# Row sums of the attention weights: one matmul group per head, or one per four heads after a fold by DMA

## The chip, the cores and the metric

The kernel runs on one core of a Trainium2 chip. The metric is the device time of one launch in microseconds (us). The core has five engines that run their own instruction streams and wait for each other by semaphores: PE (TensorE, matmuls), ACT (ScalarE), DVE (VectorE), POOL (GpSimd) and SP (SyncE, here only a queue that issues DMAs). Sixteen DMA engines move data for all queues.

## The reference

Two blocks work on the same x (2048 tokens, 1024 features) and a gate mixes them. Block A is attention with 32 heads of 32 features. Block B is a product-key expert layer. The change touches block A, and there the softmax alone.

```
g = sigmoid((x * gate_w).sum(-1, keepdims=True))
qkv = (x @ wqkv) in 3 parts, 32 heads, 32 features
scores = einsum("bhqd,bhkd->bhqk", q, k) * 32 ** -0.5
p = softmax(scores)          # exp, then divided by its sum over k
a = einsum("bhqk,bhkd->bhqd", p, v) reshaped @ wo
b = block B (keys, 8 x 8 experts, top 1)
out = g * a + (1 - g) * b
```

## The kernel before

Everything is in fp32, and where a matmul is made of two or three parts in a rounded fp32 format, in those. The first 640 us or so make q, k, v and block B's inner values and store them in HBM. The last 180 us or so multiply by wo. Between them lies the attention stage, which the change is about.

**Heads, tiles, steps.** The stage goes through 32 heads. A head's keys are cut into 16 tiles of 128 (`NT = 16`); the program calls tile `kt` of head `h` step `h * NT + kt`, and takes two steps at a time (`BT = 2`). For one step, `scores` (L968) makes four matmuls of 128 keys by 512 queries into banks of a ring of 7 PSUM banks (`ring`), and ACT takes the exponential of one to three banks at a time (L978) into an SBUF tile `P` of 128 keys by 2048 queries. Two steps later `pv` (L989) multiplies the tile by the head's values V into the PSUM bank `o`. The weight of these matmuls is 32 columns wide, so the four blocks of 512 queries go side by side, to partitions 0, 32, 64 and 96.

**Places of the tiles.** A `P` tile lives in one of eight places, `P0` to `P7`, in turn (`p_tile`). The exponential for a place waits until the tile that was there eight tiles earlier has been read by everybody.

**Row sums.** The division needs the sum of each P over all 2048 keys. Per head, `presum` adds the tiles up elementwise: tile 1 is written to `accd` directly, tiles 3, 8 and 12 are added to `accd` by accumulating DMAs that POOL issues (L1011), and DVE adds the eleven others to `acc` (L1016 and L1018). In the next head, at its step 5, `merge` adds `accd` to `acc` (L1021). At its step 8 `head_sums` sums over the 128 partitions: four matmuls with a 128 x 32 tile of ones into one bank of the ring (`rowsum`, L1002). ACT copies the bank to `ssb` (L1039), and SP stores one row of each 32 in HBM (`smd`). Once in four heads `load_r` and `norm_r` read the sums of the group back, take reciprocals times the gate (L1050, L1051) and store them (`rd`).

**The order.** It is written out by hand: the dictionary `todo` holds, for each step, the functions that run besides scores and pv. They are called after the two steps' scores and the earlier steps' pv, and before `presum` of their own step. Every engine, and every queue that issues DMAs, works in the order of the calls. SP's queue has in each head the store of the head before (`finish`, at step 0, out of `osb`), seven loads of the next head's K and Q (`load_head`, step 2), a piece of the next group's V (`load_v`, step 7) and, in heads 8 to 23, half of a row block of wo (step 11), which is needed only at the end of the kernel. POOL's queue has the three accumulating DMAs and nothing else.

**The pool `keep`.** It holds four tiles `wo_raw0` to `wo_raw3` for wo, `vhl` for block B's values and `rb0`, from before the first head on, each as large as a P tile: 8 KB in each of 128 partitions. In the heads before their loads they lie empty.

Of the kernel before, what the change touches and what calls it, by code (L numbers as in the profile page):

```python
# [9 lines left out]
F32 = mybir.dt.float32  # L10
F32R = mybir.dt.float32r
I32 = mybir.dt.int32
AF = mybir.ActivationFunctionType
OP = mybir.AluOpType
AX = mybir.AxisListType

S = 2048
D = 1024
H = 32
KC = D // 128  # L20
HC = KC // 2
NT = S // 128
NQ = S // 512
G = H // 4
W = 256
# [6 lines left out]
def gated_mha_peer_kernel(ctx, tc, xT, wqkv, wv, wo, wq, k12, ug, v, out):  # L32
# [8 lines left out]
    nc = tc.nc  # L41
# [3 lines left out]
    const = ctx.enter_context(tc.tile_pool(name="const", bufs=1))  # L45
# [10 lines left out]
    SMD = [dram.tile([4, S], F32, name=f"smd{g}") for g in range(G)]  # L56
# [3 lines left out]
    VPD = [dram.tile([128, D], F32R, name=f"vp{part}") for part in "hl"]  # L60
# [3 lines left out]
    ones = const.tile([128, 32], F32, name="ones")  # L64
# [8 lines left out]
    def dma(dst, src, queue=nc.sync):  # L73
        a, b = (ap.bitcast(F32) if ap.dtype == F32R else ap for ap in (dst, src))
        return queue.dma_start(a, b)
# [27 lines left out]
    def bank():  # L103
        i = bank_no[0] % 8
        bank_no[0] += 1
        return ps1.tile([128, 512], F32, name=f"bk{i}")
# [215 lines left out]
    for k, (w, c) in enumerate(chunks):  # L322
        hi, lo = whl.pop((w, c))
        for n in range(NQ):
            ps = bank()
# [9 lines left out]
            blk = 4 * k + n  # L335
# [16 lines left out]
            if blk >= 42 and blk < 50:  # L352
                kc = blk - 42
# [8 lines left out]

    blk = const.tile([128, 4], F32, name="blk")
    nc.vector.tensor_reduce(blk, ident.rearrange("p (j r) -> p j r", j=4), axis=AX.X, op=OP.max)
    pr = const.tile([128, KC], F32, name="pr")
    nc.vector.tensor_mul(pr, amax[:, 0, :], amax[:, 1, :])
    prm = const.tile([128, KC, 4], F32, name="prm")
# [427 lines left out]
    def values_unit(u):  # L795
# [10 lines left out]
        for k, name in enumerate(order):  # L806
# [6 lines left out]
            if last and name == "P2":  # L813
                first_scores()
# [41 lines left out]

    P, pools = {}, {}

    def p_tile(h, kt):

        i = pools["next"] % 8
        pools["next"] += 1
        P[h, kt] = pools["left" if i >= 4 else "right"].tile([128, S], F32, name=f"P{i}")
        return P[h, kt]

    def first_scores():

        tp.close()
        pools.update(right=Pool("ppr", side="right"), next=0)
        K, Q = Z  # L870
        pt = p_tile(0, 0)
        for qc, i in enumerate((5, 6, 0, 1)):
            ps = ps1.tile([128, 512], F32, name=f"bk{i}")
            c = slice(qc * 512, (qc + 1) * 512)
            nc.tensor.matmul(ps, K[:98, :128], Q[:98, c], start=True, stop=True)
            nc.scalar.activation(pt[:, c], ps, AF.Exp, scale=SCALE)
# [20 lines left out]
    xp.close()  # L897


    keep = Pool("keep")  # L900

    wo_raw = [keep.tile([128, 2, D], F32, name=f"wo_raw{i}") for i in range(KC // 2)]
    vhl = keep.tile([128, 2, D], F32R, name="vhl")
    rb0 = keep.tile([128, KC, W], F32, name="rb0")

    def raw_wo(kc):
        i, j = divmod((kc - 1) % KC, 2)
        return wo_raw[i][:, j]

    wk = Pool("wk", bufs=2)  # L910

    ACC = {0: wk.tile([128, S], F32, name="acc")}
# [10 lines left out]
    ring = pss.tile([128, NB, 512], F32, name="ring")  # L923
# [3 lines left out]
    def ring_banks(n):  # L927
        i = [(ring_no[0] + k) % NB for k in range(n)]
        ring_no[0] += n
        return i  # L930

    def on_ring(ins, *banks):

        for other, theirs in users:
            if ins.ins.engine != other.ins.engine and not theirs & set(banks):
                tc.declare_no_dep(ins.ins, other.ins, reason="different banks of the ring")
        users.append((ins, set(banks)))
        del users[:-6 * NB]
# [57 lines left out]

    SUMS = (1, 3, 8, 12), (2, 4, 6)

    def rowsum(ps, *srcs):
        for src in srcs:  # L1000
            for qc in range(NQ):
                yield nc.tensor.matmul(ps[32 * qc:32 * qc + 32, :], ones,  # L1002
                                       src[:, qc * 512:(qc + 1) * 512],
                                       start=(src is srcs[0]), stop=(src is srcs[-1]))

    def presum(h, kt):
        sums = SUMS[h == H - 1]
        if kt == 0 or kt == sums[0] or (h == H - 1 and kt >= NT - 2):
            return
        if kt in sums:  # L1010
            nc.gpsimd.dma_start(ACCD[h], P[h, kt], accum_op=OP.add)  # L1011
            return
        if kt == 1 + (sums[0] == 1):
            if h > 0:
                ACC[h] = wk.tile([128, S], F32, name="acc")
            nc.vector.tensor_add(ACC[h], P[h, 0], P[h, kt])  # L1016
        else:
            nc.vector.tensor_add(ACC[h], ACC[h], P[h, kt])  # L1018
# [4 lines left out]
    def head_sums(h):  # L1023
        i, = ring_banks(1)
        for ins in rowsum(ring[:, i, :], ACC.pop(h)):
            on_ring(ins, i)
        on_ring(norm_sums(h, ring[:, i, :]), i)

    def finish(h):
        g, j = divmod(h, 4)  # L1030
        o = wk.tile([128, 512], F32, name="osb")
        nc.scalar.activation(o, O.pop(h), AF.Copy)
        dma(OD[g][32 * j:32 * j + 32, :].rearrange("d (q s) -> q d s", q=NQ), o)


    def norm_sums(h, ps):
        g, j = divmod(h, 4)
        o = wk.tile([128, 512], F32, name="ssb")
        ins = nc.scalar.activation(o, ps, AF.Copy)  # L1039
        dma(SMD[g][j:j + 1, :].rearrange("o (q s) -> (o q) s", q=NQ), o[::32, :])  # L1040
        return ins
# [13 lines left out]
    OC, RB = {}, {}  # L1055
# [6 lines left out]

    def load_rb(n, k0, k1, js=range(4), queue=nc.sync):
        if k0 == 0 and js[0] == 0:
            RB[n] = rb0 if n == 0 else wk.tile([128, KC, W], F32, name="accd")
        for j in js:
            src = RD[k0:k1, j:j + 1, n * W:(n + 1) * W].rearrange("g j s -> j g s")
            dma(RB[n][32 * j:32 * j + 32, k0:k1, :], src.to_broadcast([32, k1 - k0, W]), queue)

    def load_chunk(n, k0, k1, queue=nc.sync):  # L1070
        load_o(n, k0, k1, queue)
        load_rb(n, k0, k1, queue=queue)
# [5 lines left out]
    def split_first(step):  # L1078
        o = OC[0][:, 0, :]
        if step == 0:  # L1080
            W0.append(zp.tile([128, 2, D], F32R, name="z1"))
            OH[0] = zp.tile([128, KC, W], F32R, name="z0")
            OL[0] = wk.tile([128, KC, W], F32R, name="acc")
            nc.vector.tensor_mul(o, o, RB[0][:, 0, :])
        elif step == 1:
            nc.scalar.activation(W0[0][:, 0], raw_wo(0), AF.Copy)
        elif step == 2:
            nc.scalar.activation(OH[0][:, 0, :], o, AF.Copy)
        else:
            for lo, src, hi in ((W0[0][:, 1], raw_wo(0), W0[0][:, 0]),  # L1090
                                (OL[0][:, 0, :], o, OH[0][:, 0, :])):
                nc.vector.tensor_tensor(out=lo, in0=src, in1=hi.bitcast(F32), op=OP.subtract)

    todo = {}

    def at(step, f, *a):
        todo.setdefault(step, []).append((f, a))

    for h in range(H):
        base = h * NT  # L1100
        g, j = divmod(h, 4)
        if h < H - 1:
            at(base + NT, finish, h)
            at(base + NT + 5, merge, h)
            at(base + NT + 8, head_sums, h)
        if j == 3 and g + 1 < G:
            at(base + NT + 10, load_r, g)
            at(base + NT + 14, norm_r, g)
        if h >= 1 and h + 1 < H:
            at(base + 2, load_head, h + 1)  # L1110
        if g + 1 < G:
            at(base + 7, load_v, g + 1, j)
# [1 line left out]
        at((H - 1) * NT + step, split_first, i)  # L1114
    at((H - 1) * NT + 13, merge, H - 1)
    for k in range(2 * KC):
        c = slice(k % 2 * D // 2, (k % 2 + 1) * D // 2)
        at((8 + k) * NT + 11, dma, raw_wo(k // 2)[:, c], wo[:, k // 2 * D:(k // 2 + 1) * D][:, c])
    for i in range(2):
        at(28 * NT + 6 + i, dma, vhl[:, i], VPD[i])  # L1120
    at(29 * NT + 13, load_o, 0, 0, 4)
    at(30 * NT + 7, load_o, 0, 4, KC - 1)
    at(30 * NT + 13, load_rb, 0, 0, KC - 1, range(2))
# [6 lines left out]
    for b0 in range(0, (H + 1) * NT, BT):  # L1130
# [9 lines left out]
        for k in range(b0, b0 + BT):  # L1140
            for f, a in todo.pop(k, []):
                f(*a)
            if now:
                presum(*now[k - b0])
    assert not todo
    pss.close()
    pools["left"].close()
    pools["right"].close()
# [29 lines left out]
    def av_mm(n, tt, half, ps, first=False, last=False):  # L1178
        for i in range(2):
            nc.tensor.matmul(ps, AT[n][:, tt * 128:(tt + 1) * 128],  # L1180
                             vhl[:, i, half * 512:(half + 1) * 512],
                             start=(first and i == 0), stop=(last and i == 1))

    bank_no = [0]
# [40 lines left out]
            nc.vector.tensor_mul(o, o, RB[n][:, k * HC:(k + 1) * HC])  # L1225
        ht.rows(OC[n])

    post = rb0.rearrange("p k m -> p (k m)").rearrange("p (a m) -> p a m", m=512)

    def plain_out(n, pa):  # L1230
        for i, ((j, half), ps) in enumerate(pa.items()):
# [44 lines left out]
    for (i, half), ps in pa.items():  # L1276
        av_mm(0, i, half, ps)
# [11 lines left out]
    for (i, half), ps in pa1.items():  # L1289
        av_mm(1, i, half, ps)  # L1290
# [127 lines left out]
```

## Time and profile before

| What | Value |
|---|---|
| median of 3 runs | 1856.39 us (1855.58 to 1862.57) |
| the profiled execution, time | 1856.62 us |
| its span, first to last instruction | 1854.8 us |
| instructions | 26123 |
| mean granted TensorE clock | 0.999 |
| PE busy | 1843.4 us, 99% |
| DVE busy | 1365.7 us, 74% |
| ACT busy | 1198.9 us, 65% |
| POOL busy | 170.1 us, 9% |

The profile is that of one execution. A row of groups has line, engine, operation, output <- inputs, shapes and count, then busy time and the mean duration of one in ns, then the idle time of the engine before them and what ended it. A row of the timeline has the start in us, the length in us, engine, line, operation and count, and in brackets the idle time before it and who ended it. A row of windows has for each engine its busy time in the stretch and the number of instructions, then the granted clock, the share of the 16 DMA engines' time that was busy, and GB/s. A row of waits has the waiting engine and line, whom it waited for, the total in us, how often, and the longest. "PEld" is the loading of weights into PE, which runs beside matmuls.

### The profile page before, as it was taken

The page shows a single profiled execution, that of the slowest core. Times are in us where ns is not written, and L with a number is a line of the kernel's source. Part 1 is how long each engine was busy: PE and PEld are TensorE (multiplying, and loading weights), DVE is VectorE, ACT ScalarE, POOL GpSimd, SP SyncE. Part 2 cuts the span into 40 slices and gives each one's busy share as a digit, 9 for nine tenths or more (in the row PEclk, how much of TensorE's full clock was granted, in tenths as well). Part 3 has the DMA queues.
Part 4 walks back from the last instruction along what each step waited for, and adds up shares of the span by engine and source line. Part 5 has one row for each costly group of instructions (what it writes and reads, how often), then busy time and mean ns, then how long its engine had stood idle before and what let it go on. Part 6 is the DMA issues. An engine that isn't in the chain of part 4 may idle for free.

```text
span 1854.8 us, 26123 instructions
## 1 busy us (share of the span) xinstructions
PE 1843.4 (99%) x10127; PEld 1130.9 (61%) x10127; DVE 1365.7 (74%) x1219; ACT 1198.9 (65%) x1492; POOL 170.1 (9%) x214
## 2 busy tenths in 40 slices
PE   9999999999999999999999999999999999999999
PEld 7877777887888744444444444444444444447787
DVE  4522224978887788888888888888888888895674
ACT  4211111201233399999999999999999999993221
POOL 0000000025401100000000000000000000000000
PEclk9999999999999999999999999999999999999999
DMA  5777784423237687767777777777777777766861
GB/s 215 281 251 255 273 290 135 134 66 104 80 127 247 246 182 160 177 153 176 163 175 176 163 183 170 184 160 183 172 172 169 159 176 177 182 147 196 273 171 57
DMA packets 122853, 332.10 MB, mean 179 GB/s; under 512 B 15988, under 2 KB 57220, under 8 KB 98472
## 3 DMA queue, kind: packets, MB, share of 16 engines
q1 hardware_dynamic: 85048, 180.58, 32.2%
q0 software_dynamic: 17584, 112.08, 28.0%
q10 hardware_dynamic: 20096, 37.76, 6.6%
q8 instruction: 80, 1.31, 0.3%
q14 instruction: 45, 0.37, 0.1%
HBM read 158.65 MB, written 72.10 MB: 124 GB/s over the span
## 4 chain that ended last, share of the span: by engine, by line
PE 85%; issue 6%; DMA 4%; DVE 3%; POOL 1%; ACT 1%; SPq 0%; ACTq 0%; DVEq 0%; POOLq 0%
PE ring L968 28%; PE o L989 25%; PE bk L329 17%; PE pa L617 6%; PE bk L394 3%; PE bk L213 2%; PE bk L274 2%; PE ring L1002 1%; DMA accd<-rd 1%; POOL eq L408 1%; PE pa L1180 1%; DMA t3l<-t2l 1%; DMA rb<-rd 1%; DMA t1l<-xl 1%; DMA smd<-ssb 0%
## 5 line engine op out<-in xcount | busy, mean ns | idle before, releaser
L978 ACT ACTIVATE P<-ring 128x1024 f32<-128x1024 f32 (+2 forms) x1031 | 913.0, 982 | 13.5 <-DMA accd<-P 1.2
L1018 DVE TENSOR_TENSOR acc<-acc,P 128x2048 f32<-128x2048 f32 x319 | 731.0, 2292 | 74.6 <-ACT P L978 49.0
L989 PE MATMUL o<-P,V 128*32 128x512 f32 x3840 | 464.8, 599 | 0.0
L968 PE MATMUL ring<-Q,K 98*128 98x512 f32 x1024 | 272.0, 407 | 0.1
L968 PE MATMUL ring<-z,z 98*128 98x512 f32 x1020 | 270.5, 407 | 0.6 <-ACT accd L978 0.6
L968 PEld LDWEIGHTS ring<-Q,K 98*128 98x128 f32 x1024 | 182.0, 188 | 144.2 <-ACT P L978 72.4
L968 PEld LDWEIGHTS ring<-z,z 98*128 98x128 f32 x1020 | 181.4, 188 | 142.5 <-ACT P L978 72.5
L989 PEld LDWEIGHTS o<-P,V 128*32 128x32 f32 x3840 | 98.8, 109 | 223.3 <-issue 214.4
L93 ACT ACTIVATE hi<-bk 128x512 fp32r<-128x512 f32 x64 | 37.6, 598 | 243.2 <-PE bk L329 227.1
L94 DVE TENSOR_TENSOR lo<-bk,hi 128x512 fp32r<-128x512 f32 x64 | 44.1, 690 | 182.7 <-ACT hi L93 178.5
L329 PE MATMUL bk<-xh,whi 128*128 128x512 f32 x448 | 176.2, 393 | 0.1
L329 PE MATMUL bk<-xh,wlo 128*128 128x512 f32 x448 | 174.4, 389 | 0.0
L329 PE MATMUL bk<-xl,whi 128*128 128x512 f32 x448 | 174.4, 389 | 0.0
L1011 POOL DMA_DIRECT2D accd<-P x95 | 81.5, 858 | 929.4 <-ACT P L978 421.4
L1016 DVE TENSOR_TENSOR acc<-P,P 128x2048 f32<-128x2048 f32 x32 | 73.4, 2293 | 72.9 <-ACT P L978 72.9
L329 PEld LDWEIGHTS bk<-xh,whi 128*128 128x128 f32 x448 | 84.1, 188 | 24.2 <-issue 6.7
L329 PEld LDWEIGHTS bk<-xh,wlo 128*128 128x128 f32 x448 | 84.1, 188 | 17.7
L329 PEld LDWEIGHTS bk<-xl,whi 128*128 128x128 f32 x448 | 84.2, 188 | 16.9
L1021 DVE TENSOR_TENSOR acc<-acc,accd 128x2048 f32<-128x2048 f32 x32 | 73.1, 2285 | 0.0
L978 ACT ACTIVATE accd<-ring 128x1024 f32<-128x1024 f32 (+2 forms) x64 | 62.2, 1032 | 2.5 <-PE ring L968 2.4
L617 PE MATMUL pa<-woh,acc 128*128 128x512 f32 x192 | 62.2, 389 | 0.0
L398 ACT ACTIVATE xu<-bk 128x64 f32<-128x64 f32 x16 | 3.6, 224 | 76.5 <-PE bk L394 71.6
(246 smaller groups left out, 1868.0 us busy)
## 6 DMA issues: line engine op xcount, KB each, us to landing
accd<-P POOLq DMA_DIRECT2D x95, 1024.0 KB, 7.5
wqt<-in_wq SPq DMA_DIRECT2D x32, 1024.0 KB
z<-kdh SPq DMA_DIRECT2D x32, 256.0 KB
z<-qdh SPq DMA_DIRECT2D x32, 256.0 KB
V<-vd SPq DMA_DIRECT2D x32, 256.0 KB
K<-kdh SPq DMA_DIRECT2D x32, 256.0 KB
Q<-qdh SPq DMA_DIRECT2D x32, 256.0 KB
od<-osb SPq DMA_DIRECT2D x32, 256.0 KB
```

Source lines behind the costliest of these rows:

```text
L93: nc.scalar.activation(hi, src, AF.Copy)
L94: (on or nc.vector).tensor_tensor(out=lo, in0=src, in1=hi.bitcast(F32), op=OP.subtract)
L329: nc.tensor.matmul(ps, a[:, kc, :], b[n][:, kc, :], start=first, stop=last)
L394: nc.tensor.matmul(ps, a[t // 4][:, kc, tok], b, start=first, stop=last)
L617: nc.tensor.matmul(ps, self.a[a][i][:, k, :], self.b[b][j][k], start=(not first and k == 0 and i == j == 0), stop=(k == HC - 1 and i == 1))
L968: on_ring(nc.tensor.matmul(ring[:, i, :], K[:98, kt * 128:(kt + 1) * 128], Q[:98, qc * 512:(qc + 1) * 512], start=True, stop=True), i)
L978: on_ring(nc.scalar.activation(P[h, kt][:, q0 * 512:(q0 + m) * 512].rearrange("p (a m) -> p a m", a=m), ring[:, i:i + m, :], AF.Exp, scale ...
L989: nc.tensor.matmul(O[h][32 * qc:32 * qc + 32, :], Vt[g][:, kt, 32 * j:32 * j + 32], p[:, qc * 512:(qc + 1) * 512], start=(kt == 0), stop=( ...
L1011: nc.gpsimd.dma_start(ACCD[h], P[h, kt], accum_op=OP.add)
L1016: nc.vector.tensor_add(ACC[h], P[h, 0], P[h, kt])
L1018: nc.vector.tensor_add(ACC[h], ACC[h], P[h, kt])
L1021: nc.vector.tensor_add(ACC[h], ACC[h], ACCD[h])
```

## The change

**The fold.** For heads 0 to 27 `head_sums` is no longer called. `halve`, at step 5 of the next head, is an accumulating DMA from POOL's queue that adds partitions 64 to 127 of `acc` to partitions 0 to 63 (512 KB). `quarter`, at step 10, has DVE copy partitions 0 to 31 of `acc` into 32 partitions of a tile `FOLD`, the head's number in its group of four choosing which 32. `add_quarter`, at step 11, is a second accumulating DMA, which adds partitions 32 to 63 of `acc` to them (256 KB). After four heads `FOLD` holds 32 partial sums of each, and `group_sums`, at step 2 of the second head after the group, makes the four matmuls once, with a weight `fours` of 128 x 32 that has eight equal columns for each head, and one copy by ACT and one store by SP. `load_r` and `norm_r` follow at steps 5 and 9 there. `merge` is at step 4 instead of 5. Heads 28 to 31 have their sums as before.

**The places.** The list `places` names for each tile its place: thirteen rounds of thirteen places (P0 to P7, `rb0` and the four `wo_raw`), then five rounds of twelve, six of eleven, six of ten, five of nine and ten of eight. `vhl`'s place is that of the `FOLD` tiles.

**The loads.** wo is loaded in heads 12 to 27 instead of 8 to 23, beginning with row block 1 and ending with block 0, and block B's values at step 6 of head 29 instead of head 28.

```diff
     nc.vector.tensor_reduce(blk, ident.rearrange("p (j r) -> p j r", j=4), axis=AX.X, op=OP.max)
+    fours = const.tile([128, 4, 8], F32, name="fours")
+    nc.vector.tensor_copy(fours, blk[:, :, None].to_broadcast([128, 4, 8]))
     pr = const.tile([128, KC], F32, name="pr")
...
+    places = []
+    for rounds, spare in ((13, 5), (5, 4), (6, 3), (6, 2), (5, 1), (10, 0)):
+        places += rounds * ([f"P{i}" for i in range(8)] +
+                            ["rb0", "wo_raw3", "wo_raw2", "wo_raw1", "wo_raw0"][:spare])
     def p_tile(h, kt):
-        i = pools["next"] % 8
-        pools["next"] += 1
-        P[h, kt] = pools["left" if i >= 4 else "right"].tile([128, S], F32, name=f"P{i}")
+        place = places.pop(0)
+        pool = pools["keep" if place[0] != "P" else "left" if place >= "P4" else "right"]
+        P[h, kt] = pool.tile([128, S], F32, name=place)
         return P[h, kt]
...
         tp.close()
-        pools.update(right=Pool("ppr", side="right"), next=0)
+        pools["right"] = Pool("ppr", side="right")
         K, Q = Z
...
-    keep = Pool("keep")
-    wo_raw = [keep.tile([128, 2, D], F32, name=f"wo_raw{i}") for i in range(KC // 2)]
-    vhl = keep.tile([128, 2, D], F32R, name="vhl")
-    rb0 = keep.tile([128, KC, W], F32, name="rb0")
+    keep = pools["keep"] = Pool("keep")
+    wo_raw = {}
+    FOLD = [keep.tile([128, S], F32, name="vhl")]
...
         i, j = divmod((kc - 1) % KC, 2)
+        if i not in wo_raw:
+            wo_raw[i] = keep.tile([128, 2, D], F32, name=f"wo_raw{i}")
         return wo_raw[i][:, j]
+    def load_wo(k):
+        kc, c = (k // 2 + 1) % KC, slice(k % 2 * D // 2, (k % 2 + 1) * D // 2)
+        dma(raw_wo(kc)[:, c], wo[:, kc * D:(kc + 1) * D][:, c])
...
-    def rowsum(ps, *srcs):
+    def rowsum(ps, *srcs, weights=ones):
         for src in srcs:
             for qc in range(NQ):
-                yield nc.tensor.matmul(ps[32 * qc:32 * qc + 32, :], ones,
+                yield nc.tensor.matmul(ps[32 * qc:32 * qc + 32, :], weights,
                                        src[:, qc * 512:(qc + 1) * 512],
...
+    def halve(h):
+        nc.gpsimd.dma_start(ACC[h][:64, :], ACC[h][64:, :], accum_op=OP.add)
+    def quarter(h):
+        g, j = divmod(h, 4)
+        if j == 0 and g > 0:
+            FOLD.append(keep.tile([128, S], F32, name="vhl"))
+        nc.vector.tensor_copy(FOLD[g][32 * j:32 * j + 32, :], ACC[h][:32, :])
+    def add_quarter(h):
+        g, j = divmod(h, 4)
+        nc.gpsimd.dma_start(FOLD[g][32 * j:32 * j + 32, :], ACC.pop(h)[32:64, :], accum_op=OP.add)
+    def group_sums(g):
+        i, = ring_banks(1)
+        for ins in rowsum(ring[:, i, :], FOLD[g], weights=fours.rearrange("p j r -> p (j r)")):
+            on_ring(ins, i)
+        o = wk.tile([128, 512], F32, name="ssb")
+        on_ring(nc.scalar.activation(o, ring[:, i, :], AF.Copy), i)
+        dma(SMD[g].rearrange("j (q s) -> q j s", q=NQ), o[::8, :])
+    vhl = []
+    def load_v_parts(i):
+        if i == 0:
+            vhl.append(keep.tile([128, 2, D], F32R, name="vhl"))
+        dma(vhl[0][:, i], VPD[i])
     def finish(h):
...
         if k0 == 0 and js[0] == 0:
-            RB[n] = rb0 if n == 0 else wk.tile([128, KC, W], F32, name="accd")
+            RB[n] = wk.tile([128, KC, W], F32, name="accd") if n else \
+                keep.tile([128, KC, W], F32, name="rb0")
         for j in js:
...
             at(base + NT, finish, h)
-            at(base + NT + 5, merge, h)
-            at(base + NT + 8, head_sums, h)
+            at(base + NT + 4, merge, h)
+            if g < G - 1:
+                at(base + NT + 5, halve, h)
+                at(base + NT + 10, quarter, h)
+                at(base + NT + 11, add_quarter, h)
+            else:
+                at(base + NT + 8, head_sums, h)
         if j == 3 and g + 1 < G:
-            at(base + NT + 10, load_r, g)
-            at(base + NT + 14, norm_r, g)
+            at(base + 2 * NT + 2, group_sums, g)
+            at(base + 2 * NT + 5, load_r, g)
+            at(base + 2 * NT + 9, norm_r, g)
         if h >= 1 and h + 1 < H:
...
     for k in range(2 * KC):
-        c = slice(k % 2 * D // 2, (k % 2 + 1) * D // 2)
-        at((8 + k) * NT + 11, dma, raw_wo(k // 2)[:, c], wo[:, k // 2 * D:(k // 2 + 1) * D][:, c])
+        at((12 + k) * NT + 11, load_wo, k)
     for i in range(2):
-        at(28 * NT + 6 + i, dma, vhl[:, i], VPD[i])
+        at(29 * NT + 6 + i, load_v_parts, i)
     at(29 * NT + 13, load_o, 0, 0, 4)
```

The places in which `vhl[...]` and `rb0` are read at the end of the kernel are renamed to `vhl[0][...]` and `RB[0]`.

6 lines of the change are left out of this document (3 added, 3 removed).

## The prediction, made before the changed kernel ran

> **What bounds the kernel now.** I read the page first, for the engines and the chain that ended last.
>
> ```profile
> span 1854.8 us, 26123 instructions
> ...
> PE 1843.4 (99%) x10127; PEld 1130.9 (61%) x10127; DVE 1365.7 (74%) x1219; ACT 1198.9 (65%) x1492; POOL 170.1 (9%) x214
> ...
> PEclk9999999999999999999999999999999999999999
> ...
> PE 85%; issue 6%; DMA 4%; DVE 3%; POOL 1%; ACT 1%; SPq 0%; ACTq 0%; DVEq 0%; POOLq 0%
> ...
> L989 PE MATMUL o<-P,V 128*32 128x512 f32 x3840 | 464.8, 599 | 0.0
> L968 PE MATMUL ring<-Q,K 98*128 98x512 f32 x1024 | 272.0, 407 | 0.1
> ```
>
> PE is busy 99% of the span at the full clock, and the two matmul groups of the attention stage stood idle for 0.1 us in all. A busy PE could still hide a slower pace, so the next view is the timeline of PE around one group of row sums, with the row of line 1002 for the count.
>
> ```profile
> 1011.05 1.92 PE L989 MATMUL o<-P,V 128*32 128x512 f32 x16
> 1012.79 1.04 PE L1002 MATMUL ring<-acc,ones 128*32 128x512 f32 x8
> 1013.76 2.11 PE L968 MATMUL ring<-Q,K 98*128 98x512 f32 x8
> 1015.80 1.93 PE L989 MATMUL o<-P,V 128*32 128x512 f32 x16
> 1017.66 2.11 PE L968 MATMUL ring<-Q,K 98*128 98x512 f32 x8
> ...
> L1002 PE MATMUL ring<-acc,ones x248: 592/592/593, 691.8 to 1655.9; 128*32 128x512 f32 x124
> ```
>
> The pv block at 1015.80 hands over to scores after 1.86 us. The one at 1011.05 hands over to the row sums after 1.74, and these to scores after 0.97, so a group of row sums costs PE 2.71 - 1.86 = 0.85 us. There are 31 such groups of 8 records, and (1655.9 - 691.8) / 30 makes a head 32.1 us. Eight blocks of scores (2.04 from 1013.76 to 1015.80) and eight of pv (1.86) make 31.2 of it, the row sums the rest: PE works without a hole, and what is taken off it in this stage shortens the kernel as long as the others keep up. How near they are, a window of 200 us shows.
>
> ```profile
> 1000.00:1200.00 200.00, 200.00 (x1248) 93.43 (x1244) 170.96 (x79) 195.10 (x227) 16.30 (x19) 1.00 0.76 175
> ```
>
> In order: PE 200 us, weight loads 93, DVE 171 (85%), ACT 195 (98%), POOL 16, the clock, and the DMA engines' share, 0.76. So three others have little room.
>
> **What is taken off PE.** Of the 31 groups in the ring 28 go and 7 come (`group_sums`, of the same four matmuls). 21 x 0.85 = 17.9 us. Against the profiled execution's own 1856.62 us, 1.8 over its span and 0.2 over the median of the runs, that is 1838.8. A head without row sums then lasts 32.1 - 0.85 = 31.25 us. The clock is at its full value, so there is nothing to win or lose there.
>
> **ACT** loses the same 21 copies to `ssb`. The exponentials stay as they were, 1095 instructions, of the same three sizes in both programs.
>
> ```profile
> L1039 ACT ACTIVATE ssb<-ring x31: 598/598/603, 692.9 to 1656.5; 128x512 f32<-128x512 f32 x31
> ```
>
> Busy 195.10 of 200 is 31.3 us a head; less three quarters of 0.60 it is 30.9, under 31.25. In front of PE lie seven banks, so a delay of ACT within a head is no loss. Worth nothing by itself.
>
> **DVE** gets the copy `quarter` per head. This is one head on its timeline:
>
> ```profile
> 1064.42 2.29 DVE L1016 TENSOR_TENSOR acc<-P,P 128x2048 f32<-128x2048 f32 x1 [2.03 <-ACT P L978]
> 1068.10 2.29 DVE L1018 TENSOR_TENSOR acc<-acc,P 128x2048 f32<-128x2048 f32 x1 [1.39 <-ACT P L978]
> 1070.31 2.28 DVE L1021 TENSOR_TENSOR acc<-acc,accd 128x2048 f32<-128x2048 f32 x1
> 1072.51 21.45 DVE L1018 TENSOR_TENSOR acc<-acc,P 128x2048 f32<-128x2048 f32 x9
> 1096.52 2.29 DVE L1016 TENSOR_TENSOR acc<-P,P 128x2048 f32<-128x2048 f32 x1 [2.55 <-ACT P L978]
> ```
>
> From 1064.42 to 1096.52 are 32.1 us with 1.39 + 2.55 idle, so twelve additions take 28.2 us, 2.4 each in a row. No copy of 32 partitions by 2048 columns from SBUF to SBUF is in the trace. The nearest one-input instructions:
>
> ```profile
> L684 DVE TENSOR_SCALAR z<-z x1: 686/686/686, 516.6 to 516.6; 128x1024 f32<-128x1024 f32 x1
> ...
> L1235 DVE COPY rb<-pa 128x512 f32<-128x512 f32 x4 | 2.7, 687 | 3.5 <-DMA out<-rb 3.5
> ```
>
> L684 has half the columns and the same memory: 0.69 is a lower bound and twice it, 1.4, my value. L1235 reads PSUM; four times it, 2.75, is the upper bound. DVE then has 28.2 + 1.4 = 29.6 us in a head, and 0.2 as the share of `norm_r`'s two instructions (at most 0.8 us in one head of four): 29.8 of 31.25, or 31.2 at the upper bound. It stays under PE's pace, but its pause shrinks from 3.9 us to 1.5.
>
> [...]
>
> The copy also waits for `halve` to land, and behind it in DVE's queue stand the additions of tiles 10, 11, 13, 14 and 15, for which ACT waits through the places. Between `merge` and the copy DVE does the additions of tiles 4, 5, 6, 7 and 9: 5 x 2.4 = 12 us are the cover. Whether they suffice, POOL's queue tells.
>
> ```profile
> 1066.51 0.86 POOL L1011 DMA_DIRECT2D accd<-P  x1 [9.16 <-PE ring L968]
> 1080.64 0.86 POOL L1011 DMA_DIRECT2D accd<-P  x1 [13.27 <-ACT P L978]
> 1088.00 0.86 POOL L1011 DMA_DIRECT2D accd<-P  x1 [6.50 <-DMA accd<-P]
> 1098.61 0.86 POOL L1011 DMA_DIRECT2D accd<-P  x1 [9.75 <-PE ring L968]
> ...
> DMA to landing us min/median/max: 6.8/7.5/14.7
> ...
> 1063.20 0.88 SPq L75 DMA_DIRECT2D z<-kdh  x2
> ...
> 1066.38 0.30 SPq L75 DMA_DIRECT2D z<-shd  x1
> ```
>
> These are the DMAs of tiles 3, 8 and 12. The second waits until 1080.64, named ACT, which was long done with tile 8; it adds to the same `accd`, so it waited for the first to land, 14.1 us after its issue. That one meets the loads of K and Q, issued from 1063.20 to 1066.38. `halve` follows `merge`, some 2.5 us behind tile 3's DMA on the same queue. If it gets through with half a normal one's time more (7.5 / 2), it lands 14.1 - 2.5 + 3.8 = 15.4 us after its issue: 3.4 past the 12 us of cover, against 1.5 us of DVE's pause. But the landing hangs on the burst of loads, which PE's pace sets, while a DVE that is late asks later: a lag of 1.9 us takes the rest of the wait away and then stays. Tiles then come free 1.9 us later; with up to thirteen places that costs nothing.
>
> **POOL and the DMA engines.** Behind `halve` stands tile 8's DMA, which waits longer for tile 3's anyway; behind `add_quarter` stands tile 12's, 7.4 us after tile 8's, and the copy is done by then. In these 32 us the queue of accumulating DMAs shows
>
> ```profile
> q0 software_dynamic: 438, 3.20, 48.4%
> ```
>
> 15.5 us of all engines for 3.20 MB, 4.84 per MB. 768 KB more are 3.8 us a head. 0.76 x 32.1 = 24.4 becomes 28.2 of 31.25, a share of 0.90. At half the rate it would be 32.0, which is the first rival.
>
> **SP.** In seven heads `group_sums`' store stands ahead of the next head's K and Q and waits for ACT, some 5 us; these have most of a head in hand. The wo loads wait for a place's last tile, at least 17 steps earlier by the list: nothing. Were it late, the K and Q behind it would be late by as much.
>
> **Places.** With eight places a tile's place is asked for again after 8 x 31.25 / 16 = 15.6 us. Tile 3's exponential (a tile each 1.95 us) and its DMA take 1.95 + 14.1 = 16.05. Before, with 16.06, ACT waited in all
>
> ```profile
> ACT P L978 <- DMA accd<-P: 1.2, 3, 0.7
> ```
>
> Eight places hold from tile 400, late in head 26, and the fold runs until head 28: two heads by 0.45, I take 1.0 us in all (0 to 2). In the earlier heads a ninth place, 1.95 us, covers it. The sum is 1839.8 us.
>
> **Rivals.** First, DMA engines as the bound: a DMA on 64 or 32 partitions runs at half the rate per byte. The head lasts 32.0 us instead of 31.25, the gain is 28 x 0.1, the time 1854. For it speaks the share of 0.76 at the start, against it that the 15.5 us above are paid per byte by every engine alike. [...] The trace has no accumulating DMA on part of the partitions.
>
> Second, ACT as the bound: if its idle 4.9 us in 200, 0.8 a head, cannot shrink, the head lasts 30.9 + 0.8 = 31.7. The gain is 28 x 0.4 = 11, the time 1845. Against it: its idle time is mostly waiting for the row sums that go.
>
> Third, slower: a ring through POOL. Copy (1.4), issue of `add_quarter` and of tile 12's DMA (0.9 each), their landing (7.5 and a quarter of it, 9.4), `merge` (2.3), landing of `halve` (T), and again the copy: 14.9 + T per head. It decides when T is over 16.4 us in every head, and at a T over 17.3 the kernel is slower by 0.5%. Waiting for tile 3's and then a full 7.5 us gives T = 19.1, a head of 34.0, 27 x 2.75 = 74 more than forecast, 1914. For it: a queue in order, with DMA engines at 0.90. Against: the longest landing seen is 14.7, and a late `halve` no longer meets the loads.
>
> That the sums don't shrink can be left out: PE's order has the seven groups and the last heads' four, no more.
>
> **How the numbers follow.** Forecast 0.60 (1837 to 1845), ACT 0.12, DMA engines 0.14 (1848 to 1864), the ring 0.14 (over 1866). A change of 0.5%, 9.3 us, is about what a measurement of this kernel can tell from none: faster (under 1847.3) is 0.60 + 0.12 = 0.72, within it 0.14, slower 0.14. The range from 1836 to 1856 holds the first two and over half of the third, 0.80.
>
> **What would show it.** PE: 88 records of line 1014 in the ring (11 groups), and 31.25 us from one head's first scores to the next's. DVE: the copy at 1.4 us or less and under 2 us of waiting for `halve` per head once the first heads are past. DMA: a share near 0.90. Wrong it would be with holes in PE between blocks: ended by ACT waiting for DVE, the ring; by ACT waiting for an accumulating DMA, the engines; by ACT itself, the second rival.

## The result, and the profile after

The changed kernel takes 1910.69 us (median of 4 runs, 1897.32 to 1912.22), the kernel before on the same chip 1857.1 (1855.58 to 1862.57): a ratio of 1.0267, with a 95% interval from 1.024 to 1.0294. The forecast was 1839.8 us, in a range from 1836 to 1856. The change is 54 us slower where 17 us of gain were forecast; the prediction was wrong.

The page of the changed kernel (time 1912.22 us), with PE's busy time, the clock by fortieths of the span, the chain that ended last, and the landings of two kinds of accumulating DMA:

```profile
span 1910.4 us, 25856 instructions
...
PE 1852.7 (97%) x9959; PEld 1130.9 (59%) x9959; DVE 1398.2 (73%) x1248; ACT 1189.2 (62%) x1471; POOL 217.3 (11%) x270
...
PEclk9999999999999999999999999989998989999999
...
PE 73%; DMA 12%; issue 8%; DVE 2%; POOL 2%; ACT 1%; SPq 1%; ACTq 0%; DVEq 0%; POOLq 0%
...
accd<-P POOLq DMA_DIRECT2D x75, 1024.0 KB, 11.1
...
acc<-acc POOLq DMA_DIRECT2D x28, 512.0 KB, 13.0
```

PE does 168 matmuls less and is busy longer than before (1852.7 us instead of 1843.4), because the clock now drops in places (0.93 between 1400 and 1500 us). DMAs hold 12% of the chain instead of 4%, and a tile's accumulating DMA lands after 11.1 us instead of 7.5. Three stretches of 100 us in the attention stage (columns as in the prediction) show where it begins:

```profile
700.00:800.00 100.00, 100.00 (x616) 47.59 (x616) 87.33 (x41) 98.26 (x114) 14.23 (x17) 1.00 0.90 190
800.00:900.00 100.00, 97.36 (x584) 45.27 (x576) 82.91 (x40) 92.57 (x107) 12.27 (x15) 0.97 0.86 179
1400.00:1500.00 100.00, 88.80 (x532) 41.25 (x524) 83.45 (x39) 84.34 (x99) 11.97 (x15) 0.93 0.83 173
```

The first heads run as forecast: PE without a hole, DMA share 0.90. From 800 us on PE has holes. Head 5, from 802 us, is the first one with `group_sums`. SP's queue there:

```profile
806.69 0.52 SPq L75 DMA_DIRECT2D od<-osb  x1
811.12 0.51 SPq L75 DMA_DIRECT2D smd<-ssb  x1
811.73 0.85 SPq L75 DMA_DIRECT2D z<-kdh  x2
...
816.20 1.25 SPq L75 DMA_DIRECT2D z<-shd  x1
821.36 0.35 SPq L75 DMA_DIRECT2D rr<-smd  x1
```

and DVE's in the same head:

```profile
815.37 9.47 DVE L1030 TENSOR_TENSOR acc<-acc,P 128x2048 f32<-128x2048 f32 x4
836.42 0.55 DVE L1091 RECIPROCAL rr<-rr 128x64 f32<-128x64 f32 x1 [11.58 <-DMA rr<-smd]
837.01 0.22 DVE L1092 TENSOR_TENSOR rr<-rr,G 128x64 f32<-128x64 f32 x1
837.15 2.29 DVE L1030 TENSOR_TENSOR acc<-acc,P 128x2048 f32<-128x2048 f32 x1
839.35 1.21 DVE L1048 COPY vhl<-acc 32x2048 f32<-32x2048 f32 x1
```

The store of the group's sums waits for ACT until 811.12. K and Q, behind it, start 4.4 us later than right behind the `od` store, and `rr`'s 32 KB, issued behind their burst, land 15 us later. DVE waits 11.58 us for them, with tile 9's addition, the copy and five more additions behind. The waits of the whole stage (engine and line, whom it waited for, us in total, times, longest):

```profile
POOL acc L1042 <- DVE acc L1033: 215.5, 27, 17.2
POOL vhl L1052 <- DVE vhl L1048: 203.5, 28, 16.6
...
DVE rr L1091 <- DMA rr<-smd: 60.8, 7, 12.5
...
ACT P L990 <- DMA accd<-P: 38.9, 7, 9.7
PE ring L980 <- ACT P L990: 34.8, 10, 9.1
DVE acc L1033 <- DMA accd<-P: 29.4, 7, 9.2
...
DVE vhl L1048 <- DMA acc<-acc: 28.9, 13, 3.9
```

So DVE waits for `rr` in seven heads (60.8 us), `merge` for the DMA of tile 12 (29.4), the copy for `halve` (28.9), and in the end ACT for a place (38.9) and PE for ACT (34.8). PE's timeline at one such hole, at 858 us:

```profile
857.85 0.80 PE L980 MATMUL ring<-z,z 98*128 98x512 f32 x1 [2.64 <-ACT rb L990]
858.58 3.64 PE L1001 MATMUL o<-P,V 128*32 128x512 f32 x16
862.15 3.02 PE L980 MATMUL ring<-z,z 98*128 98x512 f32 x8
```

Behind the hole a pv block takes 3.64 us instead of 1.93 and scores 3.02 instead of 2.11. The clock's records have the attention stage at half the full clock for 61.4 us, in eight stretches that begin in or behind such holes; the kernel before has none there, and the mean clock fell from 0.999 to 0.983. Where the loss is, the PE records of the stage tell. PE's holes sum to 49.2 us. Of the 61.4 us at half clock 18.5 lie in holes, where a slow clock costs nothing, and the other 42.9, counted at half of their work (the pv block above took 3.64 us instead of 1.93), are 21.5 us, an estimate. Together that is 70.7 us, and this execution took 1912.22 - 1839.8 = 72.4 more than the forecast. So some two thirds of the loss are waiting and one third is the clock.

### The profile page after: what moved, and what is told of

It reads as the page before. It is cut to its first block, busy times and chain, and to the rows that moved or that the text cites. A ratio compares the mean times of both kernels' runs of the same rounds, so it can differ in the third digit from the quotient of the medians.

```text
span 1910.4 us, 25856 instructions
## 1 busy us (share of the span) xinstructions
PE 1852.7 (97%) x9959; PEld 1130.9 (59%) x9959; DVE 1398.2 (73%) x1248; ACT 1189.2 (62%) x1471; POOL 217.3 (11%) x270
## 3 DMA queue, kind: packets, MB, share of 16 engines
q1 hardware_dynamic: 84964, 180.58, 31.3%
## 4 chain that ended last, share of the span: by engine, by line
PE 73%; DMA 12%; issue 8%; DVE 2%; POOL 2%; ACT 1%; SPq 1%; ACTq 0%; DVEq 0%; POOLq 0%
PE ring L980 21%; PE o L1001 19%; PE bk L329 16%; PE pa L619 6%; DMA accd<-P 6%; PE bk L396 3%; PE pa L1220 2%; PE bk L213 2%; DMA z<-shd 2%; PE bk L274 1%; SPq L75 1%; DMA K<-kdh 1%; ACT P L990 1%; DMA Q<-qdh 1%; DMA accd<-rb 1%
## 5 line engine op out<-in xcount | busy, mean ns | idle before, releaser
L990 ACT ACTIVATE P<-ring 128x1024 f32<-128x1024 f32 (+2 forms) x783 | 688.2, 972 | 65.4 <-DMA accd<-P 38.9
L1030 DVE TENSOR_TENSOR acc<-acc,P 128x2048 f32<-128x2048 f32 x233 | 533.9, 2291 | 25.7 <-ACT P L990 4.7
L1001 PE MATMUL o<-P,V 128*32 128x512 f32 x2880 | 360.4, 613 | 0.0
L980 PE MATMUL ring<-z,z 98*128 98x512 f32 x1020 | 280.4, 416 | 43.8 <-ACT P L990 34.6
L1001 PEld LDWEIGHTS o<-P,V 128*32 128x32 f32 x2880 | 75.2, 110 | 173.0 <-issue 166.2
L990 ACT ACTIVATE wo_raw<-ring 128x512 f32<-128x512 f32 (+2 forms) x175 | 164.1, 1014 | 13.4 <-PE ring L980 10.5
L1030 DVE TENSOR_TENSOR acc<-acc,wo_raw 128x2048 f32<-128x2048 f32 x61 | 139.7, 2291 | 5.7 <-ACT wo_raw L990 0.7
L1023 POOL DMA_DIRECT2D accd<-P x75 | 68.0, 906 | 414.5 <-ACT P L990 256.9
L1033 DVE TENSOR_TENSOR acc<-acc,accd 128x2048 f32<-128x2048 f32 x32 | 73.2, 2287 | 39.2 <-DMA accd<-P 29.4
L1001 PE MATMUL o<-wo_raw,V 128*32 128x512 f32 x680 | 85.7, 606 | 0.0
L990 ACT ACTIVATE rb<-ring 128x512 f32<-128x512 f32 (+2 forms) x73 | 70.1, 1004 | 5.3 <-DMA accd<-rb 3.3
## 6 DMA issues: line engine op xcount, KB each, us to landing
accd<-P POOLq DMA_DIRECT2D x75, 1024.0 KB, 11.1
accd<-wo_raw POOLq DMA_DIRECT2D x15, 1024.0 KB, 12.7
```

What stands on the lines that cost most here:

```text
L980: on_ring(nc.tensor.matmul(ring[:, i, :], K[:98, kt * 128:(kt + 1) * 128], Q[:98, qc * 512:(qc + 1) * 512], start=True, stop=True), i)
L990: on_ring(nc.scalar.activation(P[h, kt][:, q0 * 512:(q0 + m) * 512].rearrange("p (a m) -> p a m", a=m), ring[:, i:i + m, :], AF.Exp, scale ...
L1001: nc.tensor.matmul(O[h][32 * qc:32 * qc + 32, :], Vt[g][:, kt, 32 * j:32 * j + 32], p[:, qc * 512:(qc + 1) * 512], start=(kt == 0), stop=( ...
L1033: nc.vector.tensor_add(ACC[h], ACC[h], ACCD[h])
```

## The experiments

Each was run beside the kernel before, which took 1855.7 to 1859.1 us.

**SP's order.** Theory A laid the loss to SP's order and the wait for `rr`, theory B to the folded DMAs.

e1_norm_later:

```diff
-            at(base + 2 * NT + 9, norm_r, g)
+            at(base + 3 * NT + 1, norm_r, g)
```

> The changed kernel with one call moved: norm_r (DVE's reciprocal and product of a group's sums) from step 9 to step 17 of the same head, eight steps later. Theory A, SP's queue: in the seven heads with group sums their store waits for ACT and stands ahead of the loads of K and Q, which therefore start 4.4 us later and meet tile 3's DMA and halve; the load of the sums stands behind them, DVE waits 11.6 us for it with everything behind it, and the lag goes on through the copy, add_quarter and tile 12's DMA. By A DVE no longer waits for the sums and the time is 1838 to 1855. Theory B, the fold's DMAs: they are dear per byte and make a ring through POOL's queue (copy, add_quarter, tile 12's DMA, merge, halve, copy) that by itself is longer than a head of 31.25 us. By B the time stays over 1890.

Measured: 1883.06 us (1878.67 to 1888.9), ratio 1.0128 (1.0102 to 1.0155). Of the 54 us over the kernel before some 28 are gone (1910.69 - 1883.06), the others stay: neither theory has it all.

e2_old_steps:

```diff
-            at(base + 2 * NT + 2, group_sums, g)
-            at(base + 2 * NT + 5, load_r, g)
-            at(base + 2 * NT + 9, norm_r, g)
+            at(base + 2 * NT + 8, group_sums, g)
+            at(base + 2 * NT + 10, load_r, g)
+            at(base + 2 * NT + 14, norm_r, g)
...
-        at(29 * NT + 6 + i, load_v_parts, i)
+        at(29 * NT + 10 + i, load_v_parts, i)
```

> The changed kernel with group_sums, load_r and norm_r at steps 8, 10 and 14 of their head instead of 2, 5 and 9 (the steps that head_sums, load_r and norm_r have in the kernel before), so that the store of the sums no longer stands ahead of the loads of K and Q; block B's values are loaded at step 10 of head 29, behind group_sums. Theory A (SP's queue): K and Q are loaded at 5.1 us in every head, DVE's wait for the sums is under 2 us a group, time 1837 to 1846. Theory B (the fold's DMAs): over 1890.

Measured: 1880.41 us (1876.94 to 1889.0), ratio 1.012 (1.0089 to 1.0152). The wait for `rr` is gone, and in most heads K and Q start as in the kernel before (5.7 us behind the head's first scores), yet the kernel is 41 us over the forecast; both theories miss. It is the base of what follows.

**The folded DMAs.** e3_no_fold_dmas has the changed kernel without the two lines that call `halve` and `add_quarter`.

> The changed kernel without halve and add_quarter: the two accumulating DMAs of each of heads 0 to 27 are left out, DVE's copy, group_sums and the places stay (the sums are those of 32 of the 128 partitions). Theory A (SP's queue): K and Q still start late in seven heads and DVE still waits there 5 to 9 us for the sums, but no ring passes the lag on: 1840 to 1855. Theory B (the fold's DMAs): 1837 to 1841, PE without holes.

Measured: 1843.43 us (1842.46 to 1844.39), ratio 0.9913 (0.9894 to 0.9933), clock 0.999. The rest of the change is a gain; without the fold DMAs the seven waits for `rr`, some 5 us each, make no hole in PE's attention stage.

e4_eight_places is e2 with eight places throughout:

```diff
-    for rounds, spare in ((13, 5), (5, 4), (6, 3), (6, 2), (5, 1), (10, 0)):
+    for rounds, spare in ((60, 0),):
```

> The kernel e2_old_steps with eight places for the tiles in all heads instead of thirteen and later fewer. Theory A (SP's queue): with its wait gone the tile of tile 3's DMA is late by 0.5 to 3 us in each of 28 heads, PE has a hole there: 1850 to 1900. If the places matter only for a lag that the sums' wait makes: the time of e2_old_steps within 4 us. By theory B: well over 1900.

Measured: 1880.62 us (1879.6 to 1881.63), ratio 1.0113 (1.0093 to 1.0134), the same as e2. Thirteen places delay the loss to later heads (head 1 lasts 32.6 us here and 31.3 in e2) and don't save it.

e5_halve_only and e6_add_quarter_only are e2 without `add_quarter` and without `halve`.

> e2_old_steps without add_quarter: the second accumulating DMA (256 KB a head) is left out, so the sums lack partitions 32 to 63. DVE's copy still waits for halve. Theory B1, the DMA engines' time: the two fold DMAs took 166 us of all engines in 28 heads (queue q0: 35.9% of 1910.4 less 28.0% of 1854.8), 5.9 a head instead of the 3.8 forecast, and with them the engines have work for 30.3 of 31.25 us; if each byte costs the same, halve alone takes 4.0 of it and the head comes to 28.4: few holes, 1842 to 1852. Theory B2, the ring through POOL's queue: without add_quarter ahead of tile 12's DMA the ring is cut: 1839 to 1846, though the copy still waits 2 to 3 us for halve.

> e2_old_steps without halve: the first accumulating DMA (512 KB a head) is left out, the sums lack partitions 64 to 127. The copy waits for no DMA. Theory B1 (the DMA engines' time): 2.0 us a head more than before, 1839 to 1844; the queue's time shows what 256 KB on 32 partitions cost: 1.2 us a head at the price of a full DMA, 2.4 at half its rate. Theory B2 (the ring through POOL): without halve the ring is 1.4 + 1.8 + 9.4 + 2.3 + 12 of DVE's own work, under 31.25, also 1839 to 1844. The two differ in e5 and e8.

Measured: 1874.22 us (1871.7 to 1876.73), ratio 1.0088 (1.0067 to 1.011), with `halve` alone; 1839.85 (1839.25 to 1840.45), ratio 0.9903 (0.9883 to 0.9923), with `add_quarter` alone. The latter is the forecast's 1839.8. For the former both theories of that time expected at most 1852: missed.

e7_pairs folds pairs of heads: DVE copies 64 partitions of `acc` at step 6, one accumulating DMA of 512 KB adds the other 64 at step 7, and the sums are made once in two heads. DVE's copy waits for no DMA.

```diff
-                at(base + NT + 5, halve, h)
-                at(base + NT + 10, quarter, h)
-                at(base + NT + 11, add_quarter, h)
+                at(base + NT + 6, copy_half, h)
+                at(base + NT + 7, add_half, h)
```

> Another fold, complete: heads go by twos. DVE copies 64 partitions of acc to the same 64 partitions of the folded tile right after merge (step 6), one accumulating DMA adds the other 64 (step 7, 512 KB), and one group of row sums serves two heads (step 4 of the head after next, behind the loads of K and Q). DVE waits for no DMA, nothing in POOL's queue waits for a late copy, 256 KB a head less are moved. PE saves 14 x 0.85 = 11.9 us: 1845 without holes. Theory B1 (the DMA engines' time): 24.4 + 4.0 = 28.4 of 31.7 us a head, 1845 to 1853. Theory B2 (the ring through POOL): no ring, 1845 to 1849. If every DMA on 64 partitions is harmful at this load whatever waits for it: over 1857.

Measured: 1887.8 us (1879.28 to 1894.93), ratio 1.0174 (1.0147 to 1.0201). Both theories miss; only the last branch, over 1857, came. The kernel is 30 us over the one before and 43 over this variant's own forecast, although no copy waits for a DMA. So the copy's wait isn't needed for the loss; 512 KB more in POOL's queue suffice.

e8_add_quarter_later was to cut the ring of the third rival.

```diff
-                at(base + NT + 11, add_quarter, h)
+                at(base + NT + 13, add_quarter, h)
```

> e2_old_steps with add_quarter at step 13 instead of 11, behind tile 12's DMA in POOL's queue; nothing is left out. Theory B2 (the ring through POOL): tile 12's DMA no longer waits for the copy, the ring is cut, 1840 to 1852. Theory B1 (the DMA engines' time): the same bytes at the same price, the queues stay long, 1868 to 1885.

Measured: 1924.96 us (1918.95 to 1928.83), ratio 1.0351 (1.033 to 1.0372). Inconclusive: `add_quarter` now lands so late that the first addition of the head after next waits for the place of `acc` (109.9 us in all), a wait of its own.

**Time for the chain, or room on the engines.** Tiles 3, 8 and 12 add to one `accd`, each DMA behind the one before; theory C said that this chain ends too late for `merge`. Theory E said that a few DMA engines are full. In the kernel before, the `od` store has 128 packets of 2 KB, with a median of 0.084 us each. From the first one's start to the last one's are 5.5 us, and 6 of them at most run at once (medians of heads 3 to 26, from the trace's packet records).

e9_od_by_rows:

```diff
-        dma(OD[g][32 * j:32 * j + 32, :].rearrange("d (q s) -> q d s", q=NQ), o)
+        for q in range(NQ):
+            dma(OD[g][32 * j:32 * j + 32, 512 * q:512 * q + 512], o[32 * q:32 * q + 32, :])
```

> Group's steps as in e2_old_steps; only finish's store of 256 KB is cut into four DMAs of 32 rows by 2 KB. Theory E (a DMA has landed only when its last packet has; the store's 128 packets of 2 KB queue on a few DMA engines just ahead of K and Q, of tile 3's DMA and of halve, and these few engines are full): halve lands 2 us or more earlier, no holes in PE, 1838 to 1848. Theory C (three DMAs add into one accd one behind the other; 8.4 us from the head's start to tile 3's issue, then landings of about 14, 8.5 and 9 us end at 39.9, where merge's place is 8.5 us into the next head of 31.25 us; whatever makes these landings longer delays merge, and halve with it, which makes the next ones longer): the load is the same, 1870 to 1890.

Measured: **1838.93 us** (1838.53 to 1839.95), ratio 0.9897 (0.9879 to 0.9916), clock 1.0. Bytes and packets are the same; K and Q, behind four issues instead of one, start later (7.4 us behind the head's first scores instead of 5.7, medians of heads 3 to 26). The whole loss is gone. From the pages, the folded DMA and the accumulating ones out of `wo_raw`'s places, first e2, then e9:

```profile
accd<-wo_raw POOLq DMA_DIRECT2D x15, 1024.0 KB, 11.5
acc<-acc POOLq DMA_DIRECT2D x28, 512.0 KB, 13.8
```

```profile
accd<-wo_raw POOLq DMA_DIRECT2D x15, 1024.0 KB, 8.4
acc<-acc POOLq DMA_DIRECT2D x28, 512.0 KB, 12.8
```

`halve` lands 1.0 us sooner, not the 2 expected, and the others 0.7 (out of `P`) to 3.1. Tile 3's DMA, the one beside the loads of K and Q, gains most: 15.8 us from issue to landing in e2, 12.7 in e9 (medians of heads 3 to 26). The waits of the copy, of `merge` and of PE in e2, then all that e9 has of them:

```profile
DVE vhl L1048 <- DMA acc<-acc: 57.1, 20, 5.3
DVE acc L1033 <- DMA accd<-P: 21.5, 4, 8.7
...
PE ring L980 <- ACT P L990: 13.8, 9, 5.0
PE ring L980 <- DMA Q<-qdh: 11.9, 2, 6.3
...
DVE acc L1033 <- DMA accd<-wo_raw: 10.2, 3, 6.0
```

```profile
DVE vhl L1048 <- DMA acc<-acc: 35.4, 28, 2.2
```

In e9 the copy waits 1.3 us a head, `merge` never, and `merge` starts 8.9 to 9.5 us behind the first scores of every head. Nearly half of PE's holes in e2 end not with ACT but with the loads of Q, at the start of two heads. In the head before each, SP's queue had stood at the store of `rd`, which waited for `norm_r` on a late DVE, with K and Q behind it: they were issued 13.9 and 10.1 us into that head. So the lag of DVE reaches PE by two ways, through the places and through SP's queue. Now windows of e5 and e9 at the same place:

```profile
1400.00:1500.00 100.00, 100.00 (x620) 46.95 (x622) 88.75 (x43) 97.94 (x113) 11.22 (x14) 1.00 0.86 191
```

```profile
1400.00:1500.00 100.00, 100.00 (x617) 47.32 (x614) 91.60 (x44) 98.09 (x115) 13.65 (x16) 1.00 0.93 198
```

The mean share of the DMA engines is 0.86 in e5, which lost 35 us, and 0.93 in e9, which lost nothing. In e6, which lost nothing either with the store as it was, it is 0.84 there. The mean over a stretch doesn't say what is late.

e10_merge_later and e11_merge_step_later give the chain more time, with the store as it was. e10's edit is shown; e11 has `merge` at 5, `halve` at 6, `quarter` and `add_quarter` at 11:

```diff
-            at(base + NT + 4, merge, h)
+            at(base + NT + 6, merge, h)
...
-                at(base + NT + 5, halve, h)
-                at(base + NT + 10, quarter, h)
-                at(base + NT + 11, add_quarter, h)
+                at(base + NT + 7, halve, h)
+                at(base + NT + 12, quarter, h)
+                at(base + NT + 12, add_quarter, h)
```

> e2_old_steps with merge at step 6 of the head after instead of 4, halve at 7 instead of 5, quarter and add_quarter at 12 instead of 10 and 11; every transfer is as large as in e2. Theory C: merge's place on VectorE is 4.4 us later (two additions of 2.2), so that the chain of three landings has 4.4 us of slack and the lag no longer grows: 1838 to 1850, no half clock. Theory E: the full engines are as full as before, 1870 to 1890. It could also gain a wait of its own: add_quarter is issued at about 28 us and lands at 36 or 37, 5 to 6 us into the head after, where add 2 of that head wants acc's place at 6.3; then the time lies between, 1850 to 1870.

> e2_old_steps with merge at step 5 (where it was before the change), halve at 6, quarter and add_quarter both at 11. Theory C: 2.2 us of slack for the chain: better than e2 by at least half of its loss, 1840 to 1862. Theory E: 1870 to 1890.

Measured: 1891.65 us (1886.01 to 1900.19), ratio 1.018 (1.0138 to 1.0222), and 1885.94 (1878.54 to 1890.75), ratio 1.0138 (1.0109 to 1.0167). Slack for the chain helps in neither (e11 lies in theory E's range, e10 a little over it); theory C falls.

e13_before_spread is the kernel before with e9's edit.

> The kernel before with finish's store cut into four DMAs of 32 rows. Theory E: tile 3's DMA, 14 us from issue to landing in the kernel before, lands in under 12 us; the time stays at 1857, since PE sets it there. Theory C: its landing stays within 1 us of what it was; the time stays too.

Measured: 1855.25 us (1853.69 to 1857.79), ratio 0.9986 (0.9976 to 0.9996). The store's packets now take 1.8 us from first to last, 16 at once. Tile 3's DMA lands 12.4 us after its issue instead of 13.7: between the two expectations. PE had not waited for it, so the store as it was costs the kernel before next to nothing.

**Is it the spread or the cut?** e14_od_in_two cuts the store too, but leaves two blocks of q in each part.

```diff
+        for q in (0, 2):
+            dst = OD[g][32 * j:32 * j + 32, 512 * q:512 * q + 1024]
+            dma(dst.rearrange("d (q s) -> q d s", q=2), o[32 * q:32 * q + 64, :])
```

> e2_old_steps with finish's store cut into two DMAs of 64 partitions, each with the 2 KB packets of two q blocks. Theory E (few engines take a DMA whose rows are given as q, then d): the packets of the store still take over 4 us from first to last, and the time stays at 1870 to 1890. Rival (it is the cut and the later start of K and Q that help): 1838 to 1860.

Measured: 1938.79 us (1923.75 to 1943.86), ratio 1.0414 (1.0364 to 1.0463). It is slower than both ranges. The packets take 9.8 us from first to last. K and Q start 6.9 us behind the head's first scores, no later than in e9 (7.4), so it isn't their start. Of these three, the fewer packets of the store run at once, the slower:

| | store, first to last packet, us | most packets at once | time, us |
|---|---|---|---|
| e14, two DMAs of 2 x 32 rows | 9.8 | 3 | 1938.79 |
| e2, one DMA of 4 x 32 rows | 5.8 | 6 | 1880.41 |
| e9, four DMAs of 32 rows | 1.8 | 17 | 1838.93 |

(Medians of heads 3 to 26.) In e14 it isn't the fold's chain that stops PE. Of its 71.2 us of holes 70.0 end with the last load of the next head's K and Q:

```profile
PE ring L980 <- DMA z<-shd: 45.1, 6, 11.9
...
PE ring L980 <- DMA Q<-shd: 24.9, 4, 10.7
```

Before the first of these holes that load was issued at 754.87 and PE went on at 777.74, 22.9 us later. Whether the loads are late because a few engines are full, or because they stand behind the store in SP's queue, no run here separates. The trace doesn't name the engine of a packet, so on how many engines each store runs is not shown; the 3, 6 and 17 packets at once are.

e15_after_by_rows is the changed kernel, its own steps kept, with e9's edit.

> The changed kernel with its own steps (group_sums at 2, load_r at 5, norm_r at 9), only finish's store cut into four DMAs of 32 rows. Theory E alone: the wait for rr stays in the seven heads, but nothing piles up behind it: 1838 to 1846. Theory A beside E (SP's order is a cause by itself, worth the 27 us that e1 gave back): 1855 to 1870.

Measured: 1854.33 us (1845.25 to 1860.49, 10 runs), ratio 0.9982 (0.9961 to 1.0003). Its waits show

```profile
DVE rr L1092 <- DMA rr<-smd: 61.8, 7, 11.7
```

The wait is all there, 61.8 us. The time lies between the two ranges. So SP's order is a cause by itself, worth 1854.33 - 1838.93 = 15.4 us, short of the 28 that e1 gave back beside the uncut store.

e16_pairs_by_rows is e7 with e9's edit.

> The variant by pairs of heads (e7_pairs) with finish's store cut into four DMAs of 32 rows. Theory E: PE saves 14 groups of 0.85 us, 11.9: 1843 to 1850, no holes. Rival (the pairs' own 512 KB DMA, put ahead of tile 8's on POOL behind VectorE's copy, makes the chain late): 1875 to 1890 as before.

Measured: 1845.04 us (1844.95 to 1846.48), ratio 0.9938 (0.9922 to 0.9955), clock 1.0, no holes: e7's loss was the same one.

## Why the prediction was wrong

**PE: right.** 21 groups of 0.85 us. e9 has 1838.93 us and e6 1839.85, against 1838.8 by PE alone and 1839.8 forecast, and e9's heads without row sums last 31.26 us (31.25).

**ACT, DVE: right.** ACT cost nothing. The copy took 1217 ns, in this row of e2's page, under my 1.4 us:

```profile
L1048 DVE COPY vhl<-acc 32x2048 f32<-32x2048 f32 x28 | 34.1, 1217 | 60.1 <-DMA acc<-acc 57.1
```

**POOL and the DMA engines: the step that failed.** "0.76 x 32.1 = 24.4 becomes 28.2 of 31.25, a share of 0.90" took the mean over sixteen engines for the load of each. The mean itself was near: 0.90 in the first heads, 0.93 in e9. But the store's packets run 6 at once at most, and e2 and e9 differ in this store alone: with the same bytes, tile 3's DMA, for which the prediction took 14.1 us, landed after 15.8 us in e2 and after 12.7 in e9. `merge`, whose wait for the DMA of tile 12 stood at nothing in the prediction's sum, waited 31.7 us in e2 and never in e9. So what decided was the store (6 of its packets at once in e2, 17 in e9) and not the mean. The time of the accumulating queue, its share times the span, rose over e3's 530.7 us (28.8% of 1842.6) by 61 us with `add_quarter`, by 96 with `halve` and by 150 with both, per head of the 28 by 2.2, 3.4 and 5.3 us:

```profile
q0 software_dynamic: 18928, 119.42, 32.2%
```

```profile
q0 software_dynamic: 19824, 126.76, 33.5%
```

```profile
q0 software_dynamic: 21168, 134.10, 36.2%
```

(e6, e5, e2). My price of 3.8 us a head was also low: 5.3 in e2, and (35.2% of 1837.9 - 530.7) / 28 = 4.2 in e9. For e9 too this is held against e3, which has the store as it was.

That a few engines are full, as theory E has it, is argued and not shown. The windows' means, 0.84 in e6, 0.86 in e5 and 0.90 in e2, have the order of the losses, none, 35 and 41 us over e6 and e9, but none of them is 1, e9's 0.93 went without a loss, and no trace tells the load of a single engine.

What a mean over the head leaves out is the moment. From 20 to 24 us behind a head's first scores the DMA share is 0.21 in the kernel before and 0.32 in e6, and 1.02 in e5, 1.03 in e2 (medians of heads 2 to 26; times of packets overlap, so it can pass 1). `halve` prolongs the burst of store and loads, and `add_quarter` alone, issued behind it, does so far less. e9 has 1.02 there too and loses nothing, so it takes the store with 6 packets at once besides to do harm.

**"A lag of 1.9 us takes the rest of the wait away and then stays"** held in e9: `halve` lands after 12.8 us instead of 15.4, the copy waits 1.3 us a head, and nothing grows. In e2 the lag did not stay: `merge` started 9.0 us behind the first scores of head 1, 10.2 in head 2, 11.8 in head 6 and 22.2 in head 9, where in e9 it started at 8.9 to 9.1 in each of these.

**SP: wrong.** "These have most of a head in hand" was nearly true of K and Q (PE waited 7.2 us for them in three holes) and left out the load behind them: `load_r`, issued behind their burst, with `norm_r` four steps on and at the head of DVE's queue. The prediction priced `norm_r` at its 0.2 us of work. It cost 60.8 us of waiting, and 15 us of time even with the store spread.

**Clock: wrong.** "There is nothing to win or lose there" held only as long as PE had no holes. A hole of 2.6 us came with 6.8 us at half clock, and by the sum above 21.5 of the 72 us are the clock's. The stretches last 3.4 to 13.7 us, in steps of 3.4. The hole before 857.85 had 2.64 us, and one of 1.95 before 993.89 came with a stretch too, while four holes of 1.05 to 1.74 us had no half clock behind them. Why the ones and not the others is not shown.

**Places.** The 1.0 us was not tested by itself; e9 lies 0.1 us over PE's own 1838.8.

**The rivals.** The third one's 1914 us is near the result, but not by its ring: in e7 no copy waits for `halve`, and the loss is there; in e9 the ring is whole, and it is not. The first one had the right resource and, for the most part, the wrong reason: in e9 the same DMAs on 64 and 32 partitions take 4.2 us a head, where half the rate per byte would be 7.6. For the one on 32 partitions it was near: e6's 256 KB took 2.2 us a head, 1.2 at the rate of a full tile and 2.4 at half of it, and e6 lost nothing. What I didn't ask was how many packets of a store that the change leaves alone run at once.

## What to carry to other kernels

The mean DMA share of 0.76 said nothing of how a single DMA goes, here 6 of the store's 128 packets at once at most: before bytes are added to a busy stage, look in the packet records for a DMA whose packets go a few at a time, and cut it so that more of them go at once, as e9 does with DMAs of 32 rows (17 at once, 1838.93 us instead of 1880.41). The store cost next to nothing for as long as PE set the pace (e13's ratio is 0.9986) and 41 us as soon as something was added. And of a load that is moved behind a burst, ask which engine has the consumer at the head of its queue: 32 KB held up DVE for 11.6 us.

## What the runs showed that was not expected

A short hole cost more than itself: 2.64 us without scores before 857.85, and 6.8 us at half clock from 857.31 on. A mean share of 0.93 over the sixteen DMA engines, held for 28 heads, went with PE without holes; 0.86 in e5, with the store uncut, did not. And a folded half of `acc`, 512 KB, took as long to land in e9 as tile 3's full 1 MB beside the same loads of K and Q, 12.8 and 12.7 us, where the median tile took 8.4.

The version e9, the changed kernel with the group's steps moved back and the store cut by rows, is the fastest one found: 1838.93 us, 1% under the kernel before and 72 us under the changed one.
